# Loading K in 8 KB rows by one transfer per head in an attention kernel bound by its DMA stream

## The chip, the cores and the metric

One core of a Trainium2 chip. The metric is the device time of one execution in microseconds (us), as a median over executions. The record calls an execution slow when it lies over 1.5% above the fastest of the same kernel, and fast otherwise; fast ones are compared with fast ones. Where the text says "one run", the state is unknown, as it cannot be told from one execution. A few numbers come from the traces' single records of DMA packets (start, duration, size), which the shown views of the profile do not print.

## The reference, cut to what matters

Two independent blocks A and B, each with its own weights and caches; all tensors are bf16.

```python
B, Sq, D = 16, 64, 640
H, Sk, Dh = 32, 512, 128
q = (x @ wq)                                  # 16 x 64 rows, split in 32 heads of 128
scores = einsum("bhqd,bhkd->bhqk", q, k_cache) * Dh ** -0.5
p = softmax(scores)
o = einsum("bhqk,bhkd->bhqd", p, v_cache)
out = o @ wo
```

K and V of both blocks are 134.2 MB each (2 x 16 x 32 x 512 x 128 x 2 B). Nothing is read twice, so 268 of the 295 MB that the kernel moves are K and V.

## The kernel before

The work is cut into 128 packs; a pack is four heads of two batches. K of a pack is loaded with the tokens on partitions (head i on partitions 32 i to 32 i + 31), transposed in 32 x 32 blocks of bf16 pairs by VectorE (1236 ns for 128x1024 fp32), and multiplied by TensorE. V has a ring of four packs, K a ring of six. SyncE issues all these loads and waits for little but free V buffers. A ring is a set of buffers used in turn.

```python
def em_LDK(e, op):                    # two transfers per pack, one per batch b
    n, b = op.idx
    src = blocks[blk][1][2 * bp + b, h:h + 4].rearrange("h (p t) d -> (h p) (t d)", t=16)
    ins = e.dma_start(kn_ring[:, n % NK, b, :], src)          # 128 rows of 4 KB
# ...
def em_KT(e, op):                     # VectorE, one transpose per batch
    dst = kt_ring[:, n % NKT, b].rearrange("p t j k two -> p (t j k two)").bitcast(F32)
    ins = e.transpose(dst, kn_ring[:, n % NK, b, :].bitcast(F32))
# ...
def em_S(e, op):                      # TensorE, the scores
    last = e.matmul(ps[64 * b:64 * b + 64, i, :], qs_ring[rows, n % NQ, f, b, :],
                    kt_ring[rows, n % NKT, b, :, f // 2, :, f % 2], ...)
```

## Time and profile before

| | before |
|---|---|
| time, median of 3 runs | 757.96 us (757.82 to 759.49) |
| moved | 295.12 MB, 405 to 409 GB/s in most slices |
| TensorE / VectorE / ScalarE / GpSimd busy | 90 / 71 / 69 / 53% |
| K transfers | 256 of 512 KB, 4 KB packets |

The prediction below shows the time line and the windows. Two more lines of the page: the chain of work that ended last (shares of the span), and the group of the score matmuls (line, engine, operation, shapes, count, busy us, mean ns of one, idle before).

```profile
PE 33%; SPq 26%; DMA 19%; POOL 9%; DVE 8%; issue 5%; ACT 0%; POOLq 0%; DVEq 0%; ACTq 0%
...
L620 PE MATMUL ps<-kt_ring,qs_ring 32*64 32x512 bf16 x4096 | 146.4, 396 | 0.0
```

The chain is spread over engines, the issuing queue and transfers: a pipeline in balance, in which the full DMA row tells what limits it. A score matmul takes 396 ns.

### The profile page before, as it was taken

How to read it: one execution, taken by the hardware profiler on the slowest of the kernel's cores; microseconds unless marked ns; L12 is line 12 of the kernel's file. 1: busy time of each engine (PE TensorE's matmuls, PEld its weight loads, DVE VectorE, ACT ScalarE, POOL GpSimd, SP SyncE). 2: the span in 40 equal slices, each digit the busy share in tenths (PEclk: the TensorE clock that was granted, in tenths of full speed). 3: DMA queues.
4: the chain of work that ended last, by engine and by line, in shares of the span. 5: the costliest groups of instructions: out<-in, count | busy, mean ns of one | idle time of the engine just before them, and what ended most of it. 6: DMA issues, size and time to landing. Idle time of an engine off the chain costs nothing.

```text
span 757.4 us, 57362 instructions
## 1 busy us (share of the span) xinstructions
PE 682.2 (90%) x26518; PEld 528.0 (70%) x26518; DVE 536.7 (71%) x818; ACT 519.6 (69%) x1559; POOL 404.6 (53%) x580
## 2 busy tenths in 40 slices
PE   4579999999999989999978999899997999999995
PEld 3457777777777767777756776677775777777773
DVE  7437777877767777687756777777675787887873
ACT  2437777777777677767756777777775677777772
POOL 5434555546864544645674455445486556455550
PEclk9979999999999999999999999999999999999997
DMA  8999999999999999999999999999999999999970
GB/s 309 394 399 405 406 406 407 406 405 407 400 395 409 407 408 406 407 407 407 406 394 401 406 407 407 406 405 405 406 403 395 406 408 407 402 409 406 407 294 16
DMA packets 99804, 295.12 MB, mean 390 GB/s; under 512 B 9264, under 2 KB 24112, under 8 KB 99760
## 3 DMA queue, kind: packets, MB, share of 16 engines
q1 hardware_dynamic: 91120, 284.20, 95.7%
q10 hardware_dynamic: 8640, 10.49, 3.8%
q14 instruction: 35, 0.29, 0.1%
q8 instruction: 9, 0.15, 0.1%
HBM read 292.03 MB, written 2.62 MB: 389 GB/s over the span
## 4 chain that ended last, share of the span: by engine, by line
PE 33%; SPq 26%; DMA 19%; POOL 9%; DVE 8%; issue 5%; ACT 0%; POOLq 0%; DVEq 0%; ACTq 0%
SPq L546 12%; POOL pn_sb L670 8%; SPq L557 8%; PE ps L705 8%; PE ps L725 8%; PE ps L597 7%; DMA kn_ring<-in_B_k_cache_dram 6%; PE ps L620 6%; DMA kn_ring<-in_A_k_cache_dram 5%; PE ps L681 5%; SPq L559 5%; DMA v_ring<-in_B_v_cache_dram 5%; DVE pT_sb L691 3%; DMA v_ring<-in_A_v_cache_dram 3%; DVE kt_ring L610 1%
## 5 line engine op out<-in xcount | busy, mean ns | idle before, releaser
L670 POOL TENSOR_SCALAR pn_sb<-p_ring,recip 128x512 bf16<-128x512 bf16 x508 | 342.3, 694 | 322.9 <-DVE recip L654 322.8
L610 DVE STREAM_TRANSPOSE kt_ring<-kn_ring 128x1024 f32<-128x1024 f32 x256 | 313.6, 1236 | 105.8 <-DMA kn_ring<-in_B_k_cache_dram 70.3
L641 ACT ACTIVATE p_ring<-ps 128x512 bf16<-128x512 f32 x512 | 298.7, 598 | 32.1 <-PE ps L620 20.3
L691 DVE COPY pT_sb<-ps 128x1024 bf16<-128x1024 bf16 x258 | 164.6, 679 | 79.5 <-PE ps L681 78.8
L705 PE MATMUL ps<-pT_sb,v_ring 32*128 32x64 bf16 (+1 forms) x14528 | 156.7, 192 | 26.2 <-DMA v_ring<-in_B_v_cache_dram 11.0
L725 PE MATMUL ps<-wo_sb,oT_sb 128*128 128x320 bf16 x1040 | 166.6, 303 | 5.9 <-issue 4.8
L597 PE MATMUL ps<-xT_ring,wqp_sb 128*128 128x128 bf16 x2560 | 166.0, 220 | 6.1 <-POOL xT_ring L586 5.8
L705 PEld LDWEIGHTS ps<-pT_sb,v_ring 32*128 32x128 bf16 (+1 forms) x14528 | 142.1, 92 | 40.6 <-DMA v_ring<-in_B_v_cache_dram 14.1
L597 PEld LDWEIGHTS ps<-xT_ring,wqp_sb 128*128 128x128 bf16 x2560 | 157.4, 114 | 13.0 <-issue 6.0
L713 ACT ACTIVATE oT_sb<-ps 128x256 bf16<-128x256 f32 x260 | 85.6, 381 | 107.0 <-PE ps L705 107.0
L620 PE MATMUL ps<-kt_ring,qs_ring 32*64 32x512 bf16 x4096 | 146.4, 396 | 0.0
L603 ACT ACTIVATE qs_ring<-ps 128x512 bf16<-128x512 f32 x128 | 76.5, 598 | 87.7 <-PE ps L597 87.6
L681 PEld LDWEIGHTS ps<-ident,pn_sb 64*128 64x128 bf16 x4128 | 70.8, 95 | 86.8 <-ACT ps L717 65.6
L725 PEld LDWEIGHTS ps<-wo_sb,oT_sb 128*128 128x128 bf16 x1040 | 91.9, 98 | 43.8 <-issue 5.4
L681 PE MATMUL ps<-ident,pn_sb 64*128 64x64 bf16 x4128 | 84.0, 191 | 26.4 <-POOL pn_sb L670 19.8
L641 ACT ACTIVATION_READ_ACCUMULATOR p_ring<-ps 128x1 f32 x512 | 105.9, 207 | 0.0
L620 PEld LDWEIGHTS ps<-kt_ring,qs_ring 32*64 32x64 bf16 x4096 | 55.1, 104 | 31.3 <-issue 0.5
L654 DVE RECIPROCAL recip<-rowsum 128x3 f32<-128x3 f32 (+1 forms) x256 | 36.1, 158 | 24.5 <-ACT p_ring L641 21.2
L717 ACT ACTIVATE ps<-zeros 128x256 f32<-128x256 bf16 x130 | 51.3, 395 | 0.0
L569 POOL COPY wqp_sb<-ws_sb 128x1280 bf16<-128x1280 bf16 x32 | 39.3, 1260 | 7.5 <-DMA ws_sb<-in_A_wq_dram 7.5
L586 POOL COPY xT_ring<-xs_sb 128x640 bf16<-128x640 bf16 x32 | 23.0, 720 | 3.6 <-PE ps L597 3.6
L576 PE MATMUL ps<-ident,xn_ring 128*128 128x128 bf16 x165 | 14.9, 222 | 4.7 <-DMA xn_ring<-in_A_x_dram 3.5
(26 smaller groups left out, 66.3 us busy)
## 6 DMA issues: line engine op xcount, KB each, us to landing
kn_ring<-in_A_k_cache_dram SPq DMA_DIRECT2D x128, 512.0 KB, 14.1
v_ring<-in_A_v_cache_dram SPq DMA_DIRECT2D x128, 512.0 KB, 13.0
kn_ring<-in_B_k_cache_dram SPq DMA_DIRECT2D x128, 512.0 KB, 15.1
v_ring<-in_B_v_cache_dram SPq DMA_DIRECT2D x128, 512.0 KB, 12.7
ws_sb<-in_B_wq_dram SPq DMA_DIRECT2D x10, 512.0 KB, 15.6
wo_sb<-in_B_wo_dram ACTq DMA_DIRECT2D x8, 640.0 KB, 10.9
ws_sb<-in_A_wq_dram SPq DMA_DIRECT2D x4, 640.0 KB, 10.1
wo_sb<-in_A_wo_dram SPq DMA_DIRECT2D x4, 640.0 KB, 12.5
```

The lines of the kernel that those rows point to most:

```text
L546: ins = e.dma_start(kn_ring[:, n % NK, b, :], src)
L597: last = e.matmul(ps[:, 1, f * 128:(f + 1) * 128], w[:, kt, f, :], xT_ring[:, xs, kt, :], start=(kt == 0), stop=(kt == KT - 1))
L603: ins = e.activation(qs_ring[:, op.idx % NQ].rearrange("p f b q -> p (f b q)"), ps[:, 1, :], ACTF.Copy, scale=scale)
L610: ins = e.transpose(dst, kn_ring[:, n % NK, b, :].bitcast(F32))
L620: last = e.matmul(ps[64 * b:64 * b + 64, i, :], qs_ring[rows, n % NQ, f, b, :], kt_ring[rows, n % NKT, b, :, f // 2, :, f % 2], start=(f = ...
L641: ins = e.activation(dst, src, ACTF.Exp, scale=1.0, accum_out=rowsum[:, h:h + 1])
L670: ins = e.tensor_scalar(dst, src, recip[:, h // 4 % NR, i:i + 1], 1.0, ALU.mult, ALU.mult)
L681: last = e.transpose(pt_bank(b)[:, 64 * c:64 * c + 64], pn_sb[rows, c, :], ident[rows, rows], tile_position=(64 * b, 0))
L691: ins = e.tensor_copy(pT_sb[:, b].rearrange("p t q -> p (t q)"), pt_bank(b))
L705: last = e.matmul(ps[:, 4 + i, 64 * b:64 * b + 64], v_ring[rows, n % NV, b, c, :], pT_sb[rows, b, c, :], start=(t == 0 and i < 2), stop=(t ...
L713: ins = e.activation(oT_sb[:, 2 * a:2 * a + 2, :], o_ps[:, 2 * a:2 * a + 2, :], ACTF.Copy)
L725: last = e.matmul(out_ps[:, s, :], oT_sb[:, i, :], wo_sb[:, 4 * j + i, s * NH0:(s + 1) * NH0], start=(j == 0 and i == 0), stop=(j == NJ - ...
```

## The change

Intent: rows of 8 KB instead of 4 KB, so that half as many packets pay the fixed cost of a packet (12 ns, my estimate from the trace before: 2 KB packets take 87.9 ns in the mean, 4 KB packets 163.6 ns). A row of 8 KB is 32 tokens of a head, so a head has 16 rows per batch, and both batches of a head fill its 32 partitions. Beside this, the 128x3 reciprocal goes ahead of the output sum on VectorE (OS 2.53 to 2.545). The diff, cut to its core:

```diff
-AT: OS=2.53
+AT: OS=2.545
 ...
-        for b in range(2):
-            add("dve", "KT", (n, b), tk, [("kn", n % cfg.NK, b)], [("kt", n % cfg.NKT, b)])
-            op = add("sp", "LDK", (n, b), tk - 0.9, [], [("kn", n % cfg.NK, b)])
+        for i in range(4):
+            op = add("sp", "LDK", (n, i), n + AT["KT"][0] - 0.9, [], [("kn", n % cfg.NK)])
 ...   (a transpose now waits for all four transfers of its pack)
         def em_LDK(e, op):
-            src = blocks[blk][1][2 * bp + b, h:h + 4].rearrange("h (p t) d -> (h p) (t d)", t=16)
-            ins = e.dma_start(kn_ring[:, n % NK, b, :], src)
+            src = blocks[blk][1][2 * bp:2 * bp + 2, h + i].rearrange("b (p t) d -> b p (t d)", t=32)
+            dst = kn_ring[32 * i:32 * i + 32, n % NK].rearrange("p a c -> p (a c)")
+            ins = e.dma_start(dst, src)
 ...
         def em_S(e, op):
-                                        kt_ring[rows, n % NKT, b, :, f // 2, :, f % 2],
+                                        kt_ring[rows, n % NKT, :, f // 2, b, :, f % 2],
 ...
         def exp_views(h):
-            if h // 4 % NJ in WIDE:
-                return src, dst
-            return (src.rearrange("q (th tl k) -> q tl k th", th=2, tl=8),
-                    dst.rearrange("q (tl k th) -> q tl k th", tl=8, th=2))
+            u = 2 if h // 4 % NJ in WIDE else 4
+            return (src.rearrange("q (u t p) -> q t p u", u=u, p=16), dst.rearrange("q (t p u) -> q t p u", p=16, u=u))
```

More of the change, by code (lines that the diff above doesn't have):

```diff
@@ L15 @@
 SUM_MAX = 2.0 ** 40
+PARTS = dict(d_v=2, d_k=4)
 class Cfg:
@@ L32 @@
               EX=(0.21, 0.32, 0.43, 0.54), RC=(0.53, 0.75), NM=(0.56, 0.69, 0.82, 0.95), NMZ=(0.54, 0.55, 0.56, 0.76), TR=1.2,
-              TE=(1.26, 1.39), PV=1.75, OE=(2.0, 2.06), ZO=2.11, OP=2.31, OS=2.53, LDWO=2.6, ST=3.374, WP0=-1.75, WP1=-1.6)
+              TE=(1.26, 1.39), PV=1.75, OE=(2.0, 2.06), ZO=2.11, OP=2.31, OS=2.545, LDWO=2.6, ST=3.374, WP0=-1.75, WP1=-1.6)
 class Op:
@@ L141, in build_plan @@
         add("act", "QE", n, n + AT["QE"], [], [("SB", 1), ("qs", n % cfg.NQ)])
+        for i in range(4):
+            op = add("sp", "LDK", (n, i), n + AT["KT"][0] - 0.9, [], [("kn", n % cfg.NK)])
+            loads.append((n - cfg.NV + AT["PV"] + 0.2 - cfg.KLEAD, 2, op))
         for b in range(2):
             tk = n + AT["KT"][b]
-            add("dve", "KT", (n, b), tk, [("kn", n % cfg.NK, b)], [("kt", n % cfg.NKT, b)])
-            op = add("sp", "LDK", (n, b), tk - 0.9, [], [("kn", n % cfg.NK, b)])
-            loads.append((n - cfg.NV + AT["PV"] + 0.2 - cfg.KLEAD, 2, op))
+            add("dve", "KT", (n, b), tk, [("kn", n % cfg.NK)], [("kt", n % cfg.NKT, b)])
         add("pe", "S", n, n + AT["S"], [("qs", n % cfg.NQ), ("kt", n % cfg.NKT, 0), ("kt", n % cfg.NKT, 1)],
@@ L342, in finish @@
                     c2[s2] = v2
-        if op.sem[0] == "d_v" and op.count % 2 == 0:
-            for s2, v2 in self.snap[(op.sem, op.count - 1)].items():
+        part = PARTS.get(op.sem[0], 1)
+        for k in range(op.count - 1, (op.count - 1) // part * part, -1):
+            for s2, v2 in self.snap[(op.sem, k)].items():
                 if c2.get(s2, 0) < v2:
@@ L350, in wait_count @@
 def wait_count(d):
-    return d.count + d.count % 2 if d.sem[0] == "d_v" else d.count
+    part = PARTS.get(d.sem[0], 1)
+    return -(-d.count // part) * part
 def order_waits(progs, need, base):
@@ L456, in mha_kernel @@
         kn_ring = sb("kn_ring", [128, NK, 2, 2048], BF16)
-        kt_ring = sb("kt_ring", [128, NKT, 2, 16, 2, 32, 2], BF16)
+        kt_ring = sb("kt_ring", [128, NKT, 32, 2, 2, 16, 2], BF16)
         v_ring = sb("v_ring", [128, NV, 2, 16, DH], BF16)
@@ L542, in em_LDK @@
         def em_LDK(e, op):
-            n, b = op.idx
+            n, i = op.idx
             blk, bp, j, h = pack_info(n)
-            src = blocks[blk][1][2 * bp + b, h:h + 4].rearrange("h (p t) d -> (h p) (t d)", t=16)
-            ins = e.dma_start(kn_ring[:, n % NK, b, :], src)
+            src = blocks[blk][1][2 * bp:2 * bp + 2, h + i].rearrange("b (p t) d -> b p (t d)", t=32)
+            dst = kn_ring[32 * i:32 * i + 32, n % NK].rearrange("p a c -> p (a c)")
+            ins = e.dma_start(dst, src)
             return ins, ins
@@ L607, in em_KT @@
         def em_KT(e, op):
-            n, b = op.idx
-            dst = kt_ring[:, n % NKT, b].rearrange("p t j k two -> p (t j k two)").bitcast(F32)
-            ins = e.transpose(dst, kn_ring[:, n % NK, b, :].bitcast(F32))
+            n, a = op.idx
+            dst = kt_ring[:, n % NKT, 16 * a:16 * a + 16].rearrange("p t j b k two -> p (t j b k two)").bitcast(F32)
+            ins = e.transpose(dst, kn_ring[:, n % NK, a, :].bitcast(F32))
             return ins, ins
```

## The prediction

In the prediction, k is the number of DMA engines that a transfer runs on. In the trace before, every K transfer has 128 rows outermost, and there are 16 completion writes for each transfer (9264 for 579); that two batches outermost put K on two engines (k = 2) was my assumption, which that trace could not test. The lower end of the range, 2800 us, rests on nothing that a trace of this case shows.

> **What bounds the kernel now.** I read the page's time line first, then the DMA queues, the windows by stage, the queue's own waits, and last the groups of instructions on VectorE and GpSimd. The time line of the kernel before:
>
> ```profile
> PE   4579999999999989999978999899997999999995
> DVE  7437777877767777687756777777675787887873
> PEclk9979999999999999999999999999999999999997
> DMA  8999999999999999999999999999999999999970
> GB/s 309 394 399 405 406 406 407 406 405 407 400 395 409 407 408 406 407 407 407 406 394 401 406 407 407 406 405 405 406 403 395 406 408 407 402 409 406 407 294 16
> DMA packets 99804, 295.12 MB, mean 390 GB/s; under 512 B 9264, under 2 KB 24112, under 8 KB 99760
> q1 hardware_dynamic: 91120, 284.20, 95.7%
> ```
>
> The DMA row is 9 in 37 slices together, while VectorE stays at about 7. The GB/s row is flat at 405 to 409 whatever the engines do. 295.12 MB at 406 GB/s are 727 us, so 30 us of the 757.4 us span are start and end, and all the rest is the stream of K and V. The "under 512 B" number (9264) will matter below: these are the completion writes of the transfers, not data.
>
> The windows of 100 us show it again: TensorE varies between 90 and 98%, the DMA rate does not.
>
> ```profile
> core 0: us, PE busy (x) PEld busy (x) DVE busy (x) ACT busy (x) POOL busy (x), PEclk, DMA share, GB/s
> 400.00:500.00 100.00, 91.04 (x3620) 70.97 (x3618) 71.93 (x112) 71.53 (x215) 50.37 (x75) 1.00 1.03 405
> 600.00:700.00 100.00, 96.94 (x3808) 75.56 (x3793) 79.20 (x119) 74.07 (x226) 53.13 (x80) 1.00 1.03 407
> ```
>
> The share of 1.03 is a mean over 16 engines: every DMA engine is full and packet records overlap by about 3%. A kernel in this state gets slower when any engine gets more than a sixteenth of the bytes. Finally the queue's own waits and the K issues:
>
> ```profile
> SPq L557 <- PE ps L705: 54.9, 35, 5.3
> SPq L559 <- PE ps L705: 30.4, 10, 4.1
> ```
> ```profile
> L546 SPq DMA_DIRECT2D kn_ring<-in_A_k_cache_dram x128: 432/992/7372, 2.0 to 358.4; - x128
> DMA to landing us min/median/max: 6.1/14.6/20.6
> ```
>
> SyncE waits 85 us in all for free V buffers; its K issues take 0.43 us at least but 0.99 us in the median, [...]transfers land 14.6 us after issue, about 6 MB deep at 406 GB/s.
>
> [...]
> 1. [...]The trace before fits k = 16 for all: the issue list has 579 transfers, and 579 x 16 = 9264, the number of small packets.
> 2. [...]
> 3. [...]The trace shows 406 GB/s, 25.4 GB/s per engine.
> 4. [...]2 KB takes 87.9 ns in the mean, 4 KB 163.6 ns, thus 75.7 ns for each further 2 KB and 12 ns fixed.
>
> **The change part by part.**
>
> *The K transfers.* Before: two per pack of four heads, one per batch, 128 rows of 4 KB; source and destination both [128 rows]. After: four per pack, one per head. The destination is 32 partitions of 8 KB. The source, as built, has three dimensions: 2 batches (4 MB apart), 16 rows, 8 KB. The two batches cannot be merged with the rows because heads lie between them. So the slowest dimensions are 2 and 32[...]. This is the step that decides.
>
> Bytes: K is 2 x 16 x 32 x 512 x 128 x 2 B = 134.2 MB, 67.1 MB for each of two engines. The other 160.9 MB stay on 16 engines, 10.1 MB each.[...]
>
> Time of one such engine by packets, from the records before:
> - K: 67.1 MB / 8 KB = 8192 packets. One 8 KB packet[...]: 163.6 + 2 x 75.7 = 315 ns. 8192 x 315 ns = 2580 us.
> - the rest: 4 KB packets (59264 - 32768 of K) / 16 = 1656 x 163.6 ns = 271 us; 2 KB 1024 x 87.9 ns = 90 us; 1280 B 768 x 57.1 ns = 44 us; 1 KB 160 x 52.3 ns = 8 us; completion writes about 7 us. Together 420 us.
> - Sum 3000 us. Records overlap by 3% (share 1.03), so 3000 / 1.03 = 2913 us. With 30 us of start and end: 2943 us.
>
> The cross-check by rate: 77.2 MB at 25.4 GB/s is 3039 us, and 3069 us with start and end. This does not know that 8 KB packets have less fixed cost.[...] I take 2960 us.
>
> Do these two engines ever run dry? [...]V(n) lands after K(n+2); its product frees the V buffer that SyncE waits for. By then K of about four later packs, each 0.5 MB per engine or some 20 us, is allowed by the six K buffers. The compute behind a landing (transposes 2 x 1.24 us, scores, exponentials 4 x 0.6 us, product) is well under that. So they stay busy.
>
> *Twice the K issues.* 512 instead of 256, at 0.43 to about 0.65 us each: 333 us at most on SyncE in a span of 2960 us. Beside the stream.
>
> *The transposes.* Still two per pack of 128x1024, 1236 ns, but each needs all four transfers of the pack, since a half of the row now holds both batches:
>
> ```profile
> L610 DVE STREAM_TRANSPOSE kt_ring<-kn_ring 128x1024 f32<-128x1024 f32 x256 | 313.6, 1236 | 105.8 <-DMA kn_ring<-in_B_k_cache_dram 70.3
> L641 ACT ACTIVATE p_ring<-ps 128x512 bf16<-128x512 f32 x512 | 298.7, 598 | 32.1 <-PE ps L620 20.3
> L654 DVE RECIPROCAL recip<-rowsum 128x3 f32<-128x3 f32 (+1 forms) x256 | 36.1, 158 | 24.5 <-ACT p_ring L641 21.2
> ```
>
> The first transpose loses its half-pack head start, about 1.3 us (0.5 MB at 406 GB/s), where K is early anyway. The exponentials now reorder columns in every pack. Before, one pack in four did so, and all four kinds took 597 ns in the trace, so this is 0. The score matmuls read as many columns with the same step: 0.
>
> *The reciprocal ahead of the output sum.* The order of VectorE shows one swap per group of four packs: the 128x3 reciprocal (0.17 us) now precedes the 0.81 us copy or sum. 32 x 0.81 = 26 us of earlier normalisation on GpSimd at most, 32 x 0.17 = 5 us of later release. GpSimd is idle 47%; neither is on the path of the stream. 0.
>
> **The rivals.**
> A, *all 16 engines take part*: the transfer is split along the 32 destination rows, or flattened ahead of the queue. For it: somebody also tuned the order of a 0.17 us reciprocal, which fits a kernel that is near its bound. Against it: [...]the built pattern has the 2 outermost. Then K packets go from two of 163.6 to one of 315 ns, 12 ns for each of 16384 / 16 = 1024 packets per engine, 12 us; 256 more transfers cost 256 x 9.5 ns = 2 us per engine. About 747 us, within 2%.
> B, *two engines, but faster or slower*: nothing shows what one engine gives when the others are idle. [...]a loss of 5% on long rows[...] makes 3090 us.
> C, *the two engines run dry*, because [...]SyncE waits for V. Each dry spell of 3 us per pack would add 128 x 3 = 384 us, 3340 us. The six K buffers speak against it.
> D, *TensorE becomes the bound*: 682 us busy in 2960 us, no, even at half its pace.
>
> **Range and chances.** 2960 us with B's two ends gives 2800 to 3140 us. Rival A has 7 in 100, nearly all of it "same": 92% slower, 6% within 2%, 2% faster. The swap and the row size decide only inside A.
>
> **What would show each step.** For k = 2: packets under 512 B fall to 9264 - 256 x 16 + 512 x 2 = 6192; for k = 16 they rise to 9264 + 4096 = 13360. DMA digits of 2 to 3 instead of 9 ((2 x 1 + 14 x 0.13) / 16 = 0.24), about 100 GB/s flat, K landing many tens of us after issue, and the transposes waiting for K as the longest wait. 8 KB packets should record about 315 ns. VectorE, ScalarE and GpSimd keep their durations per instruction. Wrong if the DMA row is still 9 at 400 GB/s (A), or if the GB/s row saws up and down (C).

## The result, and the profile after

| | before | changed |
|---|---|---|
| time, median of 4 runs | 758.35 us (757.82 to 759.49) | 3203.99 us (3182.03 to 3208.22) |
| ratio of fast runs (6 of the changed kernel, 3161.85 to 3208.22 us) | | 4.208, 95% interval 4.180 to 4.236 |
| rate over the span | 390 GB/s | 93 GB/s |

A ratio is the mean time of one kernel's fast runs over that of the other's of the same rounds, so it is not quite the ratio of the medians. The time line and the queue of the changed kernel, 80 us per slice:

```profile
PEclk8666666666666666666666666666666666666666
DMA  3332222223322322332332232222323222222222
GB/s 106 106 107 97 87 86 98 85 93 97 103 84 92 96 92 93 96 98 85 100 100 85 90 99 86 91 90 85 100 96 98 84 91 91 86 86 94 86 86 84
DMA packets 80350, 295.13 MB, mean 93 GB/s; under 512 B 6192, under 2 KB 21040, under 8 KB 63920
q1 hardware_dynamic: 71664, 284.19, 27.0%
```

The same bytes, but the mean busy share of the 16 engines fell from full to 2 or 3 tenths. The small packets are 6192, exactly the number foretold for K on two engines. The packet records, which name no engine, agree: from the first K packet to the last, 3148 us, at most two are in flight for 3103 us, while the kernel before has 16 or more data packets in flight for 712 of its 757 us. The count of completion writes, 2 for each K transfer instead of 16, thus goes with the number of engines.

What waits is the other end. These are the chain that ended last, the queue's own wait for V buffers (total us, times, longest), the K issues (duration min/median/max in ns), and the groups of the transpose, the exponential and the reciprocal:

```profile
SPq 95%; DMA 3%; issue 1%; PE 1%; DVE 0%; ACT 0%; DVEq 0%
```
```profile
SPq L564 <- PE ps L710: 2.0, 1, 2.0
```
```profile
L553 SPq DMA_DIRECT2D kn_ring<-in_A_k_cache_dram x256: 615/4577/11940, 2.0 to 1538.9; - x128
```
```profile
L617 DVE STREAM_TRANSPOSE kt_ring<-kn_ring 128x1024 f32<-128x1024 f32 x256 | 303.5, 1224 | 2654.8 <-DMA kn_ring<-in_B_k_cache_dram 1336.4
L646 ACT ACTIVATE p_ring<-ps 128x512 bf16<-128x512 f32 x512 | 298.2, 597 | 381.0 <-DMA xn_ring<-in_B_x_dram 152.5
L659 DVE RECIPROCAL recip<-rowsum 128x3 f32<-128x3 f32 (+1 forms) x256 | 29.8, 146 | 0.3 <-ACT p_ring L646 0.2
```

SyncE hardly waits for V buffers any more (2 us instead of 85): it stands in the K issues, whose median went from 0.99 to 4.58 us; what holds an issue up is not shown. The transposes idle 2654.8 us for K, and nothing on the engines became longer: 1224, 597 and 146 ns. Only TensorE slowed (its score matmul from 396 to 591 ns, at a mean granted clock of 0.64 instead of 0.99); with 920 us busy in 3180 us it costs nothing.

So the direction and the place are as foretold. The time is not: 3204 us lies 64 us above the range. The trace's packet records say where. In the table, mean ns of one packet by size:

| run | 2 KB | 4 KB | 8 KB (K) |
|---|---|---|---|
| before | 88 | 164 | - |
| changed | 116 | 221 | 335 |

I sorted the 16384 K packets of the changed kernel by what else was in flight, on average over each one's time:

| in flight beside the K packet | K packets | mean ns |
|---|---|---|
| no other data | 11003 | 313.5 |
| only inputs and weights in 1 KB and 1280 B packets | 1136 | 339 |
| fewer than five packets of 2 or 4 KB (nearly all V), none of those | 2079 | 349 |
| five or more of 2 or 4 KB | 1949 | 440 |

(The 217 packets left over had a few of both kinds beside them.) Undisturbed, a K packet records 309 ns in the median and the next starts 306 ns after it. The 306 ns are as foretold, but in part by luck: the record is 309 and not 315 ns, and the overlap 1% and not 3%; the two errors cancel. While five or more packets, nearly all of V, are in flight, K packets take 440 ns. For all but 21 us at least one K packet is in flight, so the pair of engines does not run dry together.

### The profile page after: what moved, and what is told of

Read it like the earlier page. It is cut to its first block, busy times and chain, and to the rows that moved or that the text cites. A ratio compares the mean times of both kernels' runs of the same rounds, so it can differ in the third digit from the quotient of the medians.

```text
span 3180.3 us, 57618 instructions
## 1 busy us (share of the span) xinstructions
PE 920.0 (29%) x26518; PEld 672.4 (21%) x26518; DVE 507.3 (16%) x818; ACT 519.1 (16%) x1559; POOL 404.0 (13%) x580
## 2 busy tenths in 40 slices
DMA packets 80350, 295.13 MB, mean 93 GB/s; under 512 B 6192, under 2 KB 21040, under 8 KB 63920
## 4 chain that ended last, share of the span: by engine, by line
SPq 95%; DMA 3%; issue 1%; PE 1%; DVE 0%; ACT 0%; DVEq 0%
SPq L553 69%; SPq L564 16%; SPq L566 7%; SPq L537 2%; DMA kn_ring<-in_B_k_cache_dram 1%; DMA v_ring<-in_B_v_cache_dram 1%; DMA kn_ring<-in_A_k_cache_dram 1%; SPq L529 1%; SPq L545 0%; PE ps L710 0%; DVE kt_ring L617 0%; PE ps L730 0%; DVE pT_sb L696 0%; PE ps L627 0%; PE ps L686 0%
## 5 line engine op out<-in xcount | busy, mean ns | idle before, releaser
L710 PE MATMUL ps<-pT_sb,v_ring 32*128 32x64 bf16 (+1 forms) x14528 | 242.1, 234 | 1990.9 <-DVE pT_sb L696 703.7
L617 DVE STREAM_TRANSPOSE kt_ring<-kn_ring 128x1024 f32<-128x1024 f32 x256 | 303.5, 1224 | 2654.8 <-DMA kn_ring<-in_B_k_cache_dram 1336.4
L710 PEld LDWEIGHTS ps<-pT_sb,v_ring 32*128 32x128 bf16 (+1 forms) x14528 | 224.1, 124 | 2011.4 <-DMA v_ring<-in_B_v_cache_dram 921.3
L627 PE MATMUL ps<-kt_ring,qs_ring 32*64 32x512 bf16 x4096 | 231.9, 591 | 0.0
L730 PE MATMUL ps<-wo_sb,oT_sb 128*128 128x320 bf16 x1040 | 182.8, 324 | 3.5 <-issue 2.5
L604 PE MATMUL ps<-xT_ring,wqp_sb 128*128 128x128 bf16 x2560 | 180.9, 231 | 5.5 <-POOL xT_ring L593 5.5
L604 PEld LDWEIGHTS ps<-xT_ring,wqp_sb 128*128 128x128 bf16 x2560 | 170.1, 117 | 13.9 <-issue 5.7
L686 PEld LDWEIGHTS ps<-ident,pn_sb 64*128 64x128 bf16 x4128 | 94.9, 113 | 95.9 <-ACT ps L722 90.2
L686 PE MATMUL ps<-ident,pn_sb 64*128 64x64 bf16 x4128 | 112.6, 218 | 2.1 <-issue 1.3
L627 PEld LDWEIGHTS ps<-kt_ring,qs_ring 32*64 32x64 bf16 x4096 | 72.1, 147 | 68.5 <-issue 55.4
L583 PEld LDWEIGHTS ps<-ident,xn_ring 128*128 128x128 bf16 x165 | 13.4, 116 | 258.7 <-ACT p_ring L646 253.9
```

The source lines that it names most:

```text
L604: last = e.matmul(ps[:, 1, f * 128:(f + 1) * 128], w[:, kt, f, :], xT_ring[:, xs, kt, :], start=(kt == 0), stop=(kt == KT - 1))
L617: ins = e.transpose(dst, kn_ring[:, n % NK, a, :].bitcast(F32))
L686: last = e.transpose(pt_bank(b)[:, 64 * c:64 * c + 64], pn_sb[rows, c, :], ident[rows, rows], tile_position=(64 * b, 0))
L710: last = e.matmul(ps[:, 4 + i, 64 * b:64 * b + 64], v_ring[rows, n % NV, b, c, :], pT_sb[rows, b, c, :], start=(t == 0 and i < 2), stop=(t ...
L730: last = e.matmul(out_ps[:, s, :], oT_sb[:, i, :], wo_sb[:, 4 * j + i, s * NH0:(s + 1) * NH0], start=(j == 0 and i == 0), stop=(j == NJ - ...
```

## The experiments

Two theories to begin with, on two questions. Why four times slower: K on two engines (mine), or small transfers and long rows being slow by themselves. Why 8% more than foretold: V slows the K packets (theory 1), V costs only its own packets (2), or the engines run dry (3).

**16 rows outermost.** Two of the four edited lines; in the others the order of k and b in the ring of transposed K follows. The score matmul then reads every fourth element instead of every second, a side effect that comes up again below; here TensorE is busy for 71% of the span.

```diff
-.rearrange("b (p t) d -> b p (t d)", t=32)
+.rearrange("b (p t) d -> p b (t d)", t=32)
-kt_ring[rows, n % NKT, :, f // 2, b, :, f % 2]
+kt_ring[rows, n % NKT, :, f // 2, :, b, f % 2]
```

> The changed kernel with only the order of the source's outer dimensions swapped: 16 rows outermost, then the 2 batches; still four transfers of 256 KB per pack, 8 KB rows, 32 partitions. My theory (the slowest dimensions 2 and 32 put K on two engines): now 16 and 32, all 16 engines, small packets 13360, DMA row back at 9, about 400 GB/s, 740 to 757 us. Rival (transfers to 32 partitions, or 8 KB rows, or twice the issues are slow by themselves): still far above 1000 us.

Measured: correct, 1211.77 us in the run that is the profiled one; three others, 1245.23, 1281.86 and 1293.43 us. The kernel before took 758.27.

```profile
DMA  9999999999999999999999999999999999999992
GB/s 250 256 255 241 241 242 247 258 258 259 264 265 258 251 242 248 246 248 241 254 255 255 248 245 251 240 244 245 248 253 257 231 220 231 241 240 246 247 243 92
DMA packets 87519, 295.16 MB, mean 244 GB/s; under 512 B 13360, under 2 KB 28208, under 8 KB 71088
```

The engine count is settled: one swap of two dimensions gives 13360 small packets (16 instead of 2 for each of the 512 K transfers), a full DMA row, and takes nearly 2000 us off. But my 740 to 757 us was wrong too. All engines are full and yet move 250 GB/s: a K packet now takes 533 ns, a 4 KB packet of V 268. Something other than the number of engines also costs.

**8 rows outermost.** Each transfer of the run above is cut in two by rows.

```diff
-        for i in range(4):
+        for i in range(8):
 ...
+            i, r = divmod(i, 2)
-            dst = kn_ring[32 * i:32 * i + 32, n % NK]
+            dst = kn_ring[32 * i + 16 * r:32 * i + 16 * r + 16, n % NK]      # source rows [8 * r:8 * r + 8]
```

> As the run above, but each transfer cut in two by rows, so 8 rows outermost on the source. Theory: 8 engines carry K, 134.2/8 + 10.1 = 26.8 MB each; at 26.8 GB/s and 30 us of start and end 1030 us, and up to 1130 us if these engines lose 8% as in the changed kernel. Small packets 9264 - 4096 + 1024 x 8 = 13360. Rival (any cut below 128 partitions is equally slow): about 3200 us or more; rival (number of transfers does not matter, size neither): 750 us.

Measured: correct, 1449.58 us (one run), 13360 small packets, K packets 435 ns. The number of packets fits 8 engines (8 completion writes for each of 1024 K transfers); the time is a miss by 320 us, in the same direction as above. What follows may be its cause too; no run separates it here.

**No V.** V is loaded for the first four packs only.

```diff
-            if n < 0:
+            if n < 0 or n >= NV:
                 return None, None
```

> The changed kernel with V loaded only for the first four packs (wrong result on purpose). Theory 1 (the missing 8% are K packets slowed while V comes in on the other 14 engines): 8 KB packets record a mean near 309 instead of 335 ns, time 8192 x 306 ns + about 75 us of weights + 30 us = 2610 us. Theory 2 (V costs only its own packets on the two engines, 1536 x 159 ns + 1024 x 84 ns = 330 us): K packets stay at 335 ns, about 2870 us. Theory 3 (the two engines run dry waiting for V buffers): K packets stay at 335 ns and gaps vanish, below 2870 us.

Measured: 2678.62 us (one run, wrong result), K packets at a mean of 315 ns. Theory 1: without V the packets return to 315 ns, and the time is 191 us below theory 2's. It is 68 us above my figure: 8192 K packets at 315 instead of 309 ns alone take 49 us more, as the weights still disturb them (339 ns beside inputs and weights in the table above, 313.5 ns alone).

**Only the reciprocal moved.** The kernel before with OS at 2.545.

```diff
-OS=2.53
+OS=2.545
```

> The kernel before with only the reciprocal moved ahead of the output sum on VectorE. Both theories: within 0.3% of 758 us, as the DMA stream sets the pace; if VectorE's order mattered, up to 26 us (3%) faster.

Measured: correct, 757.94 us; ratio 0.9998, interval 0.9978 to 1.0018. The order on VectorE costs and gains nothing that can be seen.

**What else differs?** The kernel before wrote K to 128 partitions at a time, the change writes 32 neighbouring ones. I had not looked at this before predicting. So a destination theory: 32 neighbouring partitions are written slowly, 32 that are spread over all 128 are not. The next two kernels have one and the same source pattern, one dimension of 32 rows of 8 KB, and differ in the destination alone. In both expectations the first figures are the destination theory's.

**Every fourth partition.**

```diff
-            src = blocks[blk][1][2 * bp:2 * bp + 2, h + i].rearrange("b (p t) d -> b p (t d)", t=32)
-            dst = kn_ring[32 * i:32 * i + 32, n % NK]
+            src = blocks[blk][1][2 * bp + i // 2, h + 2 * (i % 2):h + 2 * (i % 2) + 2].rearrange("h (p t) d -> (h p) (t d)", t=32)
+            dst = kn_ring[i:128:4, n % NK]
```

> Four K transfers per pack, each 32 rows of 8 KB from one batch and two neighbouring heads[...], into every fourth partition (wrong result on purpose). [...]about 740 to 757 us, 8 KB packets near 315 ns. Source theory (8 KB rows or 256 KB transfers are read slowly): about 1210 to 1290 us and 530 ns, as in the run with 16 rows outermost.

Measured: 750.79 us (one run), K packets 315 ns, 4 KB packets 163 ns. K lands on wrong partitions here; the comparison still passed, since with these inputs the scores are so small (a standard deviation of 0.001) that the softmax is nearly flat.

**32 neighbouring partitions.** The same source lines, with the destination as in the change.

```diff
-            dst = kn_ring[i:128:4, n % NK]
+            dst = kn_ring[32 * i:32 * i + 32, n % NK]
```

> The same source pattern as the run into every fourth partition, but into 32 neighbouring partitions (wrong result on purpose); only the destination differs. [...]1210 to 1290 us, 8 KB packets near 530 ns. Source theory in the form that the two batches, 4 MB apart, were the cause: now 740 to 757 us; in the form that 8 KB rows are: as the other run, whatever that is.

Measured: 1267.26 us (one run), K packets 558 ns, 4 KB packets 277 ns. The DMA and GB/s rows, of the run with every fourth partition and then of this one:

```profile
DMA  8999999999999999999999999999999999999960
GB/s 316 398 402 410 412 411 413 412 411 411 406 398 414 413 412 412 413 414 413 411 400 407 410 412 411 413 412 410 412 408 400 412 414 411 413 413 411 413 264 14
```
```profile
DMA  9999999999999999999999999999999999999991
GB/s 231 239 261 243 240 240 241 242 240 239 246 242 245 246 233 240 239 237 236 241 241 234 233 234 250 227 225 224 211 217 234 235 240 240 256 253 227 231 246 50
```

Both have every engine full and the same 87519 packets, yet 412 against 240 GB/s. It is the destination: not the row length, not the transfer's size, not the distance of the two batches, which are now in separate transfers. What it is about neighbouring partitions is not shown; other steps with this source were not run. A full DMA row does not say that the engines move data at their rate (412 and 240 GB/s under the same row of nines); it says that they have a packet in hand. The mean ns of a packet says the rest (K: 315 and 558 ns).

V slows as well, though it is written to 128 partitions as before: its 4 KB packets take 268 ns in the 16-row kernel and 277 ns here, against 163 ns in the run into every fourth partition. What share of the 1212 and 1267 us this makes I have not separated.

**Does the place of V also explain the slowed K packets of the changed kernel?** The destination theory then asks for undisturbed K packets where V lands in other partitions than K; a memory theory, that V's bursts slow the reads of K, asks for the same wherever V lands. In the first two expectations the destination theory's figures come first. Three kernels with K on two engines, all wrong, with K in partitions 64 to 127 only and a smaller V. (V and K buffers are zeroed at the start; the K ring is three packs deep.) They differ in where V goes, from how many engines, and how much of it: the third loads half as many bytes of V as the first two. The numbers of V engines are my estimates, from the 16 completion writes for each transfer of the kernel before and the 8 in the run with 8 rows outermost.

```diff
+            dst = kn_ring[64 + 32 * (i % 2):96 + 32 * (i % 2), n % NK + NK * (i // 2)]        # K, all three
+            e.dma_start(v_ring[VLO:VLO + 64, n % NV], ...)       # V: 64 rows of 2 x 4 KB, 16 engines; VLO = 0, then 64
+            e.dma_start(v_ring[0:32, n % NV, b], ...)            # V in the third: 32 rows of 4 KB, 8 engines
```

> The changed kernel (K on two engines), with K written to partitions 64 to 127 only and half of V, in 4 KB packets, to partitions 0 to 63 only (wrong result on purpose). [...]8 KB packets stay near 309 ns, mean at most 315. Memory theory (V's burst slows the reads of K): mean as in the run with V in partitions 64 to 127, some 325 ns. The time is not the question (2600 to 2850 us in both).

> As the run before, but V goes to partitions 64 to 127, the half that K is written to (wrong result on purpose). [...]8 KB packets at a mean of 330 ns or more. Memory theory: the same mean as with V in the other half.

Measured: 2977.88 and 3053.65 us, both above the 2600 to 2850 expected; mean K packet 327 ns with V in the other half and 334 ns with V in K's half. My destination theory in this form fell: with V in the other half it asked for 315 ns at most. But the memory theory fell as well, since the means differ. Where five or more 4 KB packets were in flight on average, a K packet took 460 ns with V in the other half and 544 in the same. What both have in common is that 16 engines write V to 64 neighbouring partitions. So a new theory, a guess of mine from these two runs: V written in this way holds up other transfers, even those that write elsewhere. In the third kernel 8 engines write V, to 32 partitions. Its first figure below, at most 330 ns, is this theory's.

> K as in the two runs with K in partitions 64 to 127; V now 32 rows of 4 KB per transfer into partitions 0 to 31 by 8 engines[...] (wrong result on purpose). Where at least five 4 KB packets of V are in flight, a K packet took 460 ns with V in the other half[...] and 544 ns with V in K's half. [...]now at most 330 ns. Memory theory (V's burst itself slows the reads of K): still 400 ns or more.

Measured: 2832.78 us; K packets 315 ns in the mean, and 326 ns (930 of them) where five or more 4 KB packets are in flight. That is what the new theory asked for: nearly all slow packets are gone though V still comes in bursts. It does so at a lower rate here, so memory is read less hard (in those stretches V comes at 127 GB/s, against 191 in the run with V in the other half). But the run into every fourth partition read 412 GB/s with K packets at 315 ns, so a high rate of reading alone does not slow them. The third run changed the partitions, the number of engines and the bytes of V at once, so the theory fits all runs, but it is not isolated, and why V written in that way would hold up K is not shown.

**A correct kernel with 8 KB rows over all partitions.** One batch's four heads are 64 rows of 8 KB in one dimension. Put into every second partition, batch 0 on the even ones, they are spread over all 128 partitions, and each head still fills its own 32 partitions. The diff is against the run with 16 rows outermost; ends of lines are cut, as in the diffs above.

```diff
-        for i in range(4):
+        for i in range(2):
-            src = blocks[blk][1][2 * bp:2 * bp + 2, h + i].rearrange("b (p t) d -> p b (t d)", t=32)
-            dst = kn_ring[32 * i:32 * i + 32, n % NK]
+            src = blocks[blk][1][2 * bp + i, h:h + 4].rearrange("h (p t) d -> (h p) (t d)", t=32)
+            dst = kn_ring[i:128:2, n % NK]
```

The figures of the destination theory come first.

> A correct kernel with the 8 KB rows of the change: two K transfers per pack, one per batch, each 64 rows (four heads by 16, one dimension) into every second partition[...]. [...]about 750 us, 1% faster than before, 8 KB packets near 315 ns, GB/s row near 412. Rival (the step of two partitions, or two heads' worth of 8 KB rows, costs as the 32-partition transfers did): above 1000 us.

Measured: correct, 819.02 us; ratio 1.079 (1.077 to 1.082), so neither expectation was met. K packets have a median of 309 ns and single slices reach 412 GB/s; a tail of slow packets (442 over 450 ns) lifts the mean to 327 ns, and I have not explained it. But the batches now alternate inside a head's block, so a score matmul reads every fourth element:

```profile
PE 784.8 (96%) x26518; PEld 534.4 (65%) x26518; DVE 532.0 (65%) x818; ACT 519.6 (64%) x1559; POOL 404.1 (50%) x580
L627 PE MATMUL ps<-kt_ring,qs_ring 32*64 32x512 bf16 x4096 | 259.9, 619 | 0.0
```

396 ns became 619 ns at a granted clock of 0.99, TensorE went from 682 to 785 us busy, and it is the bound. A score matmul thus takes 619 ns with a step of four elements in what it reads of the ring of transposed K (512 columns on 32 rows), and 396 ns with a step of two.

**The same, with the transpose writing its columns permuted**, so that the matmuls read as before:

```diff
-            dst = kt_ring[...].rearrange("p t j k b two -> p (t j k b two)").bitcast(F32)
+            dst = kt_ring[...].rearrange("p t j b k two -> p (t j b k two)").bitcast(F32).rearrange("p (tj b k) -> p tj k b", b=2, k=16)
```

> The run with 64 rows into every second partition was held up by the score matmuls (619 instead of 396 ns each, because they read every fourth element instead of every second); here the transpose on VectorE writes its columns permuted, so that the matmuls read as in the kernel before. Theory (the DMA then sets the pace again, with 8 KB packets at 315 ns): about 750 us, 1% faster than before, score matmuls near 390 ns. Rival (the permuted write makes the 1236 ns transpose longer; 256 of them): every 10% cost 32 us of VectorE, and from 1.9 us each VectorE is the bound, above 760 us.

Measured: correct, 752.32 us (751.80 to 755.62, 6 runs; before 757.98); ratio 0.9931, interval 0.9911 to 0.9951. That is clear of noise, though the record calls it "same", as it calls everything within 2%.

```profile
GB/s 316 399 401 410 414 410 413 411 410 413 408 398 411 415 413 412 414 412 415 411 400 407 411 412 411 413 410 410 412 409 399 411 413 412 413 413 412 408 239 14
...
L618 DVE STREAM_TRANSPOSE kt_ring<-kn_ring 128x1024 f32<-128x1024 f32 x256 | 477.0, 1941 | 25.9 <-DMA kn_ring<-in_B_k_cache_dram 21.5
...
L628 PE MATMUL ps<-kt_ring,qs_ring 32*64 32x512 bf16 x4096 | 139.5, 384 | 0.0
```

This version beats both kernels, by 0.7% over the one before. The stream runs at 408 to 415 GB/s in most slices and the matmul is back at 384 ns, but the permuted write costs 1941 instead of 1236 ns for a transpose of 128x1024 fp32: VectorE is busy 90% of the span, so the price of the DMA's 1% is that it has little slack left. The rival's threshold did not hold: at 1.94 us per transpose the kernel is still below 760 us. Since the chip's comparison cannot see K rows that are permuted, I also compared outputs in a functional simulation with query weights 200 times larger: relative deviation 0.0033 for this kernel, for the one before and for the changed one, and 0.26 for the kernel with every fourth partition, as it should be. This is not in the record of runs; repeated when this text was checked, it gave the same, and 0.0033 as well for the other kernels called correct that move K differently (16 and 8 rows outermost, and every second partition without the permuted write).

## Why the prediction was wrong, point by point

1. *K goes through two engines.* Assumed, not read from the trace before, but right, to the packet: 6192 small packets, and 13360 as soon as the dimensions are swapped. This is the step that decided, and it made the call of "slower".
2. *8192 packets of 315 ns, 306 with overlap, per engine.* This is the term that failed. Undisturbed it was right (306 ns from start to start, by the luck told above). The mean was 335 ns, so with the 3 ns of overlap 8192 x 332 = 2720 us instead of 8192 x 306 = 2507: 213 us of the 237 us by which the profiled run (3180) exceeds the 2943 of the sum. From the table of K packets, V makes about 169 us of it: (2079 x 40 + 1949 x 131) / 2 ns over 309. The prediction took the packet's duration from a kernel in which all K and V transfers wrote 128 partitions, and assumed that V on other engines leaves K packets alone. That V lengthens them is shown: without V their mean is 315 ns. Why it does is inferred: the three runs with K in the upper half (460, 544 and 326 ns) fit V writes that hold up K even where it writes elsewhere, but the third changed more than one thing, and the changed kernel's trace does not record where a packet goes.
3. *The other packets, 420 us or 408 with overlap.* Not measured by itself; by difference 3180 - 30 - 2720 = 430 us.
4. *The engines do not run dry (rival C).* Held: in the trace before, V(n) landed 2.4 to 4.6 us after K(n+2) (packs 10 to 119), as the argument has it; in the changed kernel at least one K packet is in flight for all but 21 us, and SyncE waits 2 us for V buffers. The sign that the prediction named for C would have misled: the GB/s row does go up and down, between 84 and 107.
5. *Rival B named the gap*, that nothing showed what an engine gives when others are idle, but bounded the loss at 5%. It was 8% (3180 against 2943 us).
6. *Rival A, 16 engines, about 747 us.* Wrong in a way that mattered only for the experiments: 16 engines into 32 neighbouring partitions take 1212 to 1267 us. The 747 us hold only where the rows are spread over all partitions too (751 us).
7. *Twice the issues, the transposes, exponentials and the reciprocal beside the stream: 0.* Right; the reciprocal alone gave 0.9998. (The prediction's "flat at 405 to 409" overlooks single slices at 394 to 403; nothing rests on it.)

## What to carry to other kernels

Before changing a DMA's shape, look at two things: its outermost dimension as built, and how its partitions lie. Here 2, 8 and 16 outermost in the source of K gave 2, 8 and 16 completion writes for each transfer; with two, no more than two K packets were in flight for 3103 of 3148 us, and the kernel took 3204 us. And 16 engines into 32 neighbouring partitions took 1267 us (240 GB/s over the mix with V), into every fourth 751 us (412 GB/s). A wide step over partitions can spread a short list of long rows: 32 rows into every fourth partition had K packets of 315 ns, 64 rows into every second 309 ns in the median. And when a rate is carried from one profile to another, ask whether its conditions come along: here a K packet of 8 KB took 309 to 315 ns without V, or with K spread over all partitions, and 335 ns in the changed kernel.
